# A scan's phase carried from chunk to chunk by an addition into the input's last row, in place of a small transfer or a selecting product

## The chip, the core and the metric

The kernel runs on one core of a Trainium2 chip. The metric is the time of one execution on the device, in microseconds (us). Five engines work side by side, each in its own order: PE (TensorE, products), DVE (VectorE), ACT (ScalarE), POOL (GpSimd) and SP (SyncE, which issues most transfers).

## What is computed

A gated linear attention with complex decay, and on its output a mixture of experts with one expert per token.

```
mag = sqrt(a_re^2 + a_im^2);  scale = min(mag, 0.999) / (mag + 1e-6)
for t in range(768):                       # per batch (4) and head (8), head_dim 48
    S = (a_re*scale + i*a_im*scale)[t] * S + outer(k[t], v[t])
    y[t] = q[t] @ real(S)
x = y as rows: 3072 tokens x 384
e = argmax(x @ w_gate);  out = softmax gate * sigmoid(x @ w_output_gate)[e] * (relu(x @ w1[e]) @ w2[e])
```

## The kernel before

The scan is done in chunks of 128 tokens: 4 batches of 6 chunks, 24 chunks in all, with a chunk's tokens on the 128 partitions and heads times head_dim, 384 numbers, along the row. Chunks are worked in groups (`sizes`) of 1, 1, 2, 2, 3, 3, 3, 3, 3, 3. The first four groups are the six chunks of the first batch.

For a chunk the kernel needs the running sum over its tokens of log magnitude (`decay`, L512) and of phase (`turns`, L560). Both are products with a constant triangle: `tri_l` at L521, `tri_t` at L574, each with 128x384 float32 data, which the trace shows as two matmul records. The phase is the arctangent of a_im / a_re, written in place into the tile `ai` by `prep_trig` (L508, which records as L234). After the product, DVE rounds (L578) and subtracts (L579), so that `ai` now holds the running phase in turns, wrapped to half a turn; L585 takes its absolute value, and `phase` (L600) takes sine and cosine of both on ACT.

The phase must go on from chunk to chunk within a batch. The last token's running phase lies in partition 127 of the finished chunk; the next chunk's first token lies in partition 0. There are two ways, by group (`CARRY = 3`):

- Chunks 1 to 5 (groups 0 to 3): after the product with `tri_t`, a second product (L576) with `sel`, a 32x128 constant that picks row 127, adds the carry to all rows in PSUM. The product with `tri_t` does not wait for the chunk before, the one with `sel` does.
- Chunks 6 to 23 (groups 4 to 9): SP moves row 127 to a tile `carry` on partition 0 (L584), and DVE adds it, times 2 pi, to partition 0 of the next chunk's `ai` (L556) before that chunk's product with `tri_t`. Chunks 6, 12 and 18 begin a batch and take no carry.

Around it, by chunk: `turn` (L618) multiplies k and q by the sines and cosines on DVE (L622, tiles `kc`, `qc`) and turns them on PE (L94, tile `tr`), ACT copies them out (L632); `score` (L657) makes scores on PE (L664) and masks them on DVE (L665); `state` (L636) and `values` (L671) make the state (L644, L649) and the output (L678, L684); `finish` (L693) makes rows and gate logits (L245). Beside them `prep_exp` (L451) prepares the magnitudes of the next group: ACT exponentials and logarithms, and DVE's L467, L481, L490 and L500 over 1152 numbers a row for a group of three.

The order of the attention's instructions is not written out by hand: the generators `main` and `side` say in what order the steps are recorded, `@urge` gives some of them a priority (`turning` counts as recorded 30 instructions earlier), and a planner then orders each engine's and each queue's instructions by priority and by when it takes them to be ready. Only the end of the attention and the experts (L1402 to L1405) are in an order fixed by hand. Each engine works through its own list in order, and an instruction that waits holds up all behind it.

In the experts' part each of the 8 experts makes its rows by products of three float32r parts (L1235, L1172).

## Time and profile before

| | |
|---|---|
| median of 3 runs | 533.52 us (533.45 to 533.83) |
| profiled execution | 535.06 us |
| its span | 533.3 us |
| PE busy | 495.2 us, 93% of the span |
| DVE busy | 340.6 us, 64% |
| ACT busy | 314.2 us, 59% |
| POOL busy | 116.3 us, 22% |

The attention takes the first 300 us or so, the experts the rest. The rows come from the profiled execution, whose time is 1.76 us above its span and 1.54 us above the median of the runs. Busy shares are averages over stages with different limits; what a change in one stage is worth is read from that stage.

### The profile page before, as it was taken

How to read it: one execution, taken by the hardware profiler on the slowest of the kernel's cores; microseconds unless marked ns; L12 is line 12 of the kernel's file. 1: busy time of each engine (PE TensorE's matmuls, PEld its weight loads, DVE VectorE, ACT ScalarE, POOL GpSimd, SP SyncE). 2: the span in 40 equal slices, each digit the busy share in tenths (PEclk: the TensorE clock that was granted, in tenths of full speed). 3: DMA queues.
4: the chain of work that ended last, by engine and by line, in shares of the span. 5: the costliest groups of instructions: out<-in, count | busy, mean ns of one | idle time of the engine just before them, and what ended most of it. 6: DMA issues, size and time to landing. Idle time of an engine off the chain costs nothing.

```text
span 533.3 us, 10970 instructions
## 1 busy us (share of the span) xinstructions
PE 495.2 (93%) x4191; PEld 427.8 (80%) x4191; DVE 340.6 (64%) x801; ACT 314.2 (59%) x581; POOL 116.3 (22%) x134
## 2 busy tenths in 40 slices
PE   2899896999989999999989899999999999999992
PEld 0378574877877878778787789999999999999992
DVE  5579678998877988898857646444353636355220
ACT  7678677887858789657624236355452726354220
POOL 4002002030110203033310544412334232111112
PEclk9799989999989999999999799999999999999998
DMA  8664542526235321104424565537163544431001
GB/s 285 199 216 137 120 132 61 164 67 179 72 75 149 45 77 49 29 31 135 143 56 145 161 170 180 165 82 235 44 205 120 173 149 142 142 115 50 15 27 45
DMA packets 46898, 63.84 MB, mean 120 GB/s; under 512 B 11769, under 2 KB 38668, under 8 KB 46836
## 3 DMA queue, kind: packets, MB, share of 16 engines
q1 hardware_dynamic: 38708, 53.63, 33.6%
q0 software_dynamic: 8128, 9.42, 6.2%
q8 instruction: 35, 0.57, 0.5%
q14 instruction: 27, 0.22, 0.2%
HBM read 53.92 MB, written 9.88 MB: 120 GB/s over the span
## 4 chain that ended last, share of the span: by engine, by line
PE 59%; issue 16%; DVE 8%; DMA 7%; ACT 5%; POOL 3%; POOLq 0%; SPq 0%; DVEq 0%; ACTq 0%
PE acc L1172 12%; PE up L1235 11%; PE tr L94 6%; PE sc L664 5%; PE cs L574 4%; PE xo L678 4%; PE tr L245 4%; PE cs L521 3%; POOL out_dram L1185 3%; PE xo L684 2%; DMA carry<-ai 2%; PE st L649 2%; DMA xd<-xn 1%; DMA ar<-in_a_re_dram 1%; DMA raw<-in_moe_w_dram 1%
## 5 line engine op out<-in xcount | busy, mean ns | idle before, releaser
L1240 DVE SCALAR_TENSOR_TENSOR hl<-up,hh 128x464 fp32r<-128x464 f32 (+7 forms) x64 | 37.7, 589 | 69.8 <-ACT hh L1239 69.5
L1239 ACT ACTIVATE hh<-up 128x464 fp32r<-128x464 f32 (+7 forms) x64 | 33.0, 516 | 72.5 <-PE up L1235 72.5
L1235 PE MATMUL up<-xh,w1h 128*128 128x464 f32 (+7 forms) x192 | 69.1, 360 | 0.2 <-ACT xh L1022 0.2
L1235 PE MATMUL up<-xl,w1h 128*128 128x464 f32 (+7 forms) x192 | 68.1, 355 | 0.0
L1235 PE MATMUL up<-xh,w1l 128*128 128x464 f32 (+7 forms) x192 | 67.8, 353 | 0.0
L1172 PE MATMUL acc<-hh,w2h 128*128 128x464 f32 (+6 forms) x168 | 61.8, 368 | 0.0
L1172 PE MATMUL acc<-hl,w2h 128*128 128x464 f32 (+6 forms) x168 | 59.8, 359 | 1.5 <-DVE hl L1240 1.5
L1172 PE MATMUL acc<-hh,w2l 128*128 128x464 f32 (+6 forms) x168 | 59.8, 356 | 0.0
L1185 POOL DMA_INDIRECT out_dram<-y,sid x28 | 31.7, 1134 | 125.2 <-ACT y L1207 122.2
L664 PE MATMUL sc<-qt,kt 96*128 96x128 f32 x384 | 52.4, 279 | 0.0
L664 PEld LDWEIGHTS sc<-qt,kt 96*128 96x128 f32 x384 | 47.2, 191 | 3.3 <-issue 1.7
L1116 POOL DMA_INDIRECT rows<-xd,sid x28 | 35.5, 1267 | 57.7 <-DVE w1l L211 29.2
L211 DVE TENSOR_TENSOR w1l<-raw,w1h 128x512 fp32r<-128x512 f32 x48 | 30.7, 685 | 18.9 <-ACT w1h L210 18.8
L678 PE MATMUL xo<-scores,v 128*48 128x128 f32 x384 | 42.7, 279 | 0.0
L211 DVE TENSOR_TENSOR w2l<-raw,w2h 128x512 fp32r<-128x512 f32 x48 | 30.6, 688 | 14.6 <-ACT w2h L210 14.3
L1062 POOL DMA_INDIRECT table<-entry,addr x20 | 28.1, 1404 | 53.5 <-DVE addr L1058 49.3
L1235 PEld LDWEIGHTS up<-xl,w1h 128*128 128x128 f32 x192 | 36.3, 189 | 1.6 <-DVE xl L1023 0.4
L210 ACT CAST w1h<-raw 128x512 fp32r<-128x512 f32 x48 | 27.1, 619 | 17.9 <-DMA raw<-in_moe_w_dram 17.9
L1235 PEld LDWEIGHTS up<-xh,w1h 128*128 128x128 f32 x192 | 36.5, 190 | 1.3 <-ACT xh L1022 0.4
L544 POOL COPY rcs<-rcs 24x48 f32<-24x48 f32 (+2 forms) x10 | 5.4, 540 | 146.2 <-DMA rcs<-re 95.6
L1235 PEld LDWEIGHTS up<-xh,w1l 128*128 128x128 f32 x192 | 36.4, 190 | 1.0
L684 PE MATMUL xo<-qt,state 96*48 96x128 f32 x320 | 36.7, 276 | 0.0
(213 smaller groups left out, 1117.9 us busy)
## 6 DMA issues: line engine op xcount, KB each, us to landing
raw<-in_moe_w_dram SPq DMA_DIRECT2D x32, 768.0 KB
ar<-in_a_re_dram SPq DMA_DIRECT2D x24, 192.0 KB
ai<-in_a_im_dram SPq DMA_DIRECT2D x24, 192.0 KB
k<-in_k_dram SPq DMA_DIRECT2D x24, 192.0 KB
q<-in_q_dram SPq DMA_DIRECT2D x24, 192.0 KB
v<-in_v_dram SPq DMA_DIRECT2D x24, 192.0 KB
xd<-xn SPq DMA_DIRECT2D x24, 192.0 KB
rows<-xd,sid POOLq DMA_INDIRECT x28, 4.3
```

Source lines behind the costliest of these rows:

```text
L94: return nc.tensor.transpose(out=out, in_=in_, identity=ident[p0:p0 + n, p0:p0 + n])
L211: nc.vector.tensor_tensor(out=lo[:, s], in0=raw[:, s], in1=hi[:, s].bitcast(F32), op=ALU.subtract)
L664: nc.tensor.matmul(sp[:, j * P:(j + 1) * P], r["kt"][:D2, h, :], r["qt"][:D2, h, :], start=True, stop=True)
L678: nc.tensor.matmul(op[u * DP:u * DP + D, j * P:(j + 1) * P], vt[c][:, h * D:(h + 1) * D], r["s"][:, h, :], start=True, stop=(cc == 0))
L684: nc.tensor.matmul(op[u * DP:u * DP + D, j * P:(j + 1) * P], xs[:D2, h * D:(h + 1) * D], r["qt"][:D2, h, :], start=False, stop=True)
L1062: ins = nc.gpsimd.indirect_dma_start(out=table, out_offset=bass.IndirectOffsetOnAxis(ap=addr[:, c:c + 1], axis=0), in_=entry[:, c, :], in_ ...
L1116: ins = nc.gpsimd.indirect_dma_start(out=rows[e % 2][:n, i, :], out_offset=None, in_=xd[:known], in_offset=bass.IndirectOffsetOnAxis(ap=id ...
L1172: nc.tensor.matmul(accs[kt][:, :cap], w[:, cs], a, start=(ft == 0 and s == 0), stop=(ft == FT - 1 and s == 2))
L1185: ins = nc.gpsimd.indirect_dma_start(out=out, out_offset=bass.IndirectOffsetOnAxis(ap=id_of(e, i, n, loaded), axis=0), in_=y[:n, :], in_of ...
L1235: nc.tensor.matmul(up[:, :cap], w[:, kt, :], x[:, kt, :], start=(m == 0), stop=(m == 3 * KT - 1))
L1239: nc.scalar.activation(out=hh, in_=up[:, :cap], func=AF.Relu)
L1240: nc.vector.scalar_tensor_tensor(out=hl, in0=up[:, :cap], scalar=0.0, in1=hh.bitcast(F32), op0=ALU.max, op1=ALU.subtract)
```

## The change

The arrays a_re and a_im are handed to the kernel with the tokens of each chunk rotated by one: rows 0 to 126 hold tokens 1 to 127, and row 127 holds token 0. The rotation is made where the inputs are laid out, outside of the measured time. The triangles are made to fit, so that the running sums come out in the tokens' own order: `tri_ring` makes a strict triangle and fills its row 127. The first token's phase then lies in partition 127, as the carry does, and one DVE instruction on partitions 96 to 127 adds it in place, with a per-partition factor `last` that is 2 pi in partition 127 and zero in the others. The transfer (L584), the tile `carry`, the product with `sel` (L576) and the constants `sel`, `tri_r` and `tri_o` go. The path taken only when a decay is too strong (`recurrence`, not run with these inputs) first copies both arrays back into the tokens' order.

```diff
-    tri_l = tri("tri_l", 0.5)
-    tri_r = const.tile([P, P], F32R, name="tri_r")
-    nc.gpsimd.tensor_copy(out=tri_r, in_=tri_l)
-    tri_t = tri("tri_t", 1.0 / (2.0 * math.pi))
+    def tri_ring(name, val):
+        t = tri(name, val, strict=True)
+        nc.gpsimd.affine_select(
+            out=t, in_=t, pattern=[[0, P]], compare_op=ALU.is_ge, fill=val, base=P - 2, channel_multiplier=-1)
+        return t
+
+    tri_l = tri_ring("tri_l", 0.5)
+    tri_t = tri_ring("tri_t", 1.0 / (2.0 * math.pi))
     mask = tri("mask", 1.0)
-    tri_o = const.tile([P, P], F32R, name="tri_o")
-    nc.gpsimd.tensor_copy(out=tri_o, in_=mask)
...
-    sel = const.tile([P, P], F32, name="sel")
-    nc.gpsimd.memset(sel, 1.0)
+    last = const.tile([P, 1], F32, name="last")
+    nc.gpsimd.memset(last, 2.0 * math.pi)
     nc.gpsimd.affine_select(
-        out=sel, in_=sel, pattern=[[0, P]], compare_op=ALU.is_ge, fill=0.0,
-        base=-(P - 1), channel_multiplier=1,
-    )
+        out=last, in_=last, pattern=[[0, 1]], compare_op=ALU.is_ge, fill=0.0, base=-(P - 1), channel_multiplier=1)
...
             def carried(g, c):
 
-                first = (starts[g] + c) % NC == 0
-                fr = G[g]["ai"][:, c, :]
-                plain = st["carry"] is not None and st["carry"].shape[0] > 1
-                if not first and not plain:
+                if (starts[g] + c) % NC:
+                    row = G[g]["ai"][96:128, c, :]
                     nc.vector.scalar_tensor_tensor(
-                        out=fr[0:1, :], in0=st["carry"], scalar=2.0 * math.pi, in1=fr[0:1, :], op0=ALU.mult, op1=ALU.add)
-                return first, plain
+                        out=row, in0=st["carry"], scalar=last[96:128], in1=row, op0=ALU.mult, op1=ALU.add)
...
                 tp = pp.tile([P, 512], F32, name="cs")
...
-                    nc.tensor.matmul(tp[:, :HD], tri_t, fr, start=True, stop=first or not plain)
-                if not first and plain:
-                    nc.tensor.matmul(tp[:, :HD], sel[96:128], st["carry"], start=False, stop=True)
+                nc.tensor.matmul(tp[:, :HD], tri_t, fr, start=True, stop=True)
...
-                if g <= CARRY:
-                    st["carry"] = fr[96:128, :]
-                else:
-                    st["carry"] = early.tile([1, HD], F32, name="carry")
-                    nc.sync.dma_start(out=st["carry"], in_=fr[127:128, :])
+                st["carry"] = fr[96:128, :]
...
+        if name in ("a_re", "a_im"):
+            a = _np.ascontiguousarray(_np.roll(a.reshape(a.shape[0], -1, P, *a.shape[2:]), -1, axis=2).reshape(a.shape))
```

The branches for `g >= SPLIT` and `g >= TSPLIT`, which no group reaches (both are 99), go as well.

## Rows read from the trace of the kernel before

**Rows 1.** The page: busy time of each engine with its share of the span and instructions, and the TensorE clock granted in 40 equal slices of 13.3 us, in tenths of full speed.
```profile
PE 495.2 (93%) x4191; PEld 427.8 (80%) x4191; DVE 340.6 (64%) x801; ACT 314.2 (59%) x581; POOL 116.3 (22%) x134
...
PEclk9799989999989999999999799999999999999998
```

**Rows 2.** The waits of the whole span: who waited for whom, us in total, times, longest us.
```profile
PE cs L574 <- DVE ai L556: 7.2, 3, 4.3
...
DVE ai L556 <- DMA carry<-ai: 5.4, 4, 2.5
```

**Rows 3.** The chain of work that ended last, in order of time: start us, length us, what. Pieces of 3 us and more from 60 to 165 us.
```profile
87.07 3.34 DMA carry<-ai
...
119.57 4.21 DMA carry<-ai
...
150.07 4.87 DMA carry<-ai
```

**Rows 4.** Busy time by stretch (us from the span's start): length, busy us and instructions of PE, PEld, DVE, ACT, POOL, then granted clock as a share of full speed, DMA share, GB/s.
```profile
80.00:95.00 15.00, 10.73 (x102) 7.09 (x99) 13.23 (x37) 10.30 (x17) 3.17 (x3) 0.89 0.30 71
...
148.00:162.00 14.00, 12.04 (x109) 10.22 (x108) 9.99 (x26) 6.23 (x12) 1.24 (x1) 0.88 0.42 93
...
180.00:210.00 30.00, 30.00 (x365) 23.28 (x363) 25.93 (x63) 25.32 (x45) 4.64 (x4) 1.00 0.28 63
...
300.00:533.00 233.00, 223.51 (x1258) 215.96 (x1256) 100.76 (x173) 101.99 (x203) 66.13 (x57) 0.98 0.41 127
```

**Rows 5.** The timeline from 85 to 94 us, PE, then DVE, then ACT: start us, length us, engine, line, operation, out<-in, count, and in brackets the idle time before it and what ended it.
```profile
91.12 1.28 PE L574 MATMUL cs<-ai,tri_t 128*128 128x384 f32 x2 [4.27 <-DVE ai L556]
92.30 1.65 PE L521 MATMUL cs<-l,tri_l 128*128 128x384 f32 x2
93.77 1.60 PE L94 MATMUL tr<-ident,kc 128*96 128x128 f32 x8
...
86.49 0.55 DVE L579 TENSOR_TENSOR ai<-cs,rnd 128x384 f32<-128x384 f32 x1
86.96 1.35 DVE L481 SCALAR_TENSOR_TENSOR lnr<-lnr,t 128x1152 f32<-128x1152 f32 x1
...
90.43 0.55 DVE L556 SCALAR_TENSOR_TENSOR ai<-carry,ai 1x384 f32<-1x384 f32 x1 [0.56 <-DMA carry<-ai]
...
92.78 0.94 DVE L622 TENSOR_TENSOR kc<-k,trig 128x768 f32<-128x768 f32 x1
...
88.34 1.25 ACT L234 ACTIVATE t<-lnr,b_eps 128x1152 f32<-128x1152 f32 x1 [3.01 <-DVE lnr L481]
...
91.34 0.60 ACT L234 ACTIVATE trig<-rnd,b_cos 128x384 f32<-128x384 f32 x1
```

**Rows 6.** The timeline from 119 to 126 us, PE, then DVE.
```profile
124.41 0.91 PE L574 MATMUL cs<-ai,tri_t 128*128 128x384 f32 x2 [0.95 <-DVE ai L556]
125.16 0.60 PE L94 MATMUL tr<-ident,qc 128*96 128x128 f32 x4
125.60 1.04 PE L245 MATMUL tr<-comb,xt 128*128 128x112 f32 x8
...
119.00 0.55 DVE L579 TENSOR_TENSOR ai<-cs,rnd 128x384 f32<-128x384 f32 x1
...
121.20 0.94 DVE L622 TENSOR_TENSOR qc<-q,trig 128x768 f32<-128x768 f32 x1
123.81 0.55 DVE L556 SCALAR_TENSOR_TENSOR ai<-carry,ai 1x384 f32<-1x384 f32 x1 [1.67 <-DMA carry<-ai]
```

**Rows 7.** The timeline from 149 to 159 us, PE, then DVE.
```profile
152.97 0.64 PE L94 MATMUL tr<-ident,qc 128*96 128x128 f32 x4
155.57 0.93 PE L574 MATMUL cs<-ai,tri_t 128*128 128x384 f32 x2 [1.96 <-DVE ai L556]
156.31 1.03 PE L94 MATMUL tr<-ident,qc 128*96 128x128 f32 x4
157.14 1.89 PE L245 MATMUL tr<-comb,xt 128*128 128x112 f32 x8
...
151.56 0.95 DVE L622 TENSOR_TENSOR qc<-q,trig 128x768 f32<-128x768 f32 x1
154.97 0.55 DVE L556 SCALAR_TENSOR_TENSOR ai<-carry,ai 1x384 f32<-1x384 f32 x1 [2.45 <-DMA carry<-ai]
```

**Rows 8.** The timeline from 15 to 27 us, PE, then DVE.
```profile
15.71 2.25 PE L574 MATMUL cs<-ai,tri_t 128*128 128x384 f32 x4 [3.05 <-POOL rcs L544]
18.09 1.61 PE L576 MATMUL cs<-ai,sel 32*128 32x384 f32 x2
...
17.38 0.56 DVE L579 TENSOR_TENSOR ai<-cs,rnd 128x384 f32<-128x384 f32 x1
...
19.74 0.56 DVE L578 TENSOR_SCALAR rnd<-cs 128x384 f32<-128x384 f32 x1 [1.41 <-PE cs L576]
```

**Rows 9.** Busy time of PE alone in two short stretches near the start: length, PE busy and instructions, granted clock, DMA share, GB/s.
```profile
20.00:23.00 3.00, 3.00 (x10) 0.50 0.66 180
...
23.00:26.00 3.00, 3.00 (x14) 0.96 0.96 322
```

**Rows 10.** Instructions that write or read the tile `carry`: count, shortest, median and longest ns, first and last start us, form.
```profile
L584 SPq DMA_DIRECT2D carry<-ai x18: 534/552/2036, 80.4 to 240.6; - x18
L556 DVE SCALAR_TENSOR_TENSOR ai<-carry,ai x15: 536/540/601, 84.0 to 237.2; 1x384 f32<-1x384 f32 x15
```

More of the change, by code (lines that the diff above doesn't have):

```diff
@@ L516, in decay @@
                     lp = pp.tile([P, 512], F32, name="cs")
[L517 to L521 removed]
+                    nc.tensor.matmul(lp[:, :HD], tri_l, d["l2"][:, c, :], start=True, stop=True)
                     re = early.tile([P, HD], F32, name="re")
@@ L550, in carried, with turns @@
             def carried(g, c):
[L552 to L555 removed]
+                if (starts[g] + c) % NC:
+                    row = G[g]["ai"][96:128, c, :]
                     nc.vector.scalar_tensor_tensor(
[L557 to L562 removed]
+                        out=row, in0=st["carry"], scalar=last[96:128], in1=row, op0=ALU.mult, op1=ALU.add)
+            def turns(g, c, taken=False):
+                if not taken:
+                    carried(g, c)
                 fr = G[g]["ai"][:, c, :]
                 tp = pp.tile([P, 512], F32, name="cs")
[L565 to L576 removed]
+                nc.tensor.matmul(tp[:, :HD], tri_t, fr, start=True, stop=True)
                 rnd = early.tile([P, HD], F32, name="rnd", bufs=4)
@@ L579, in turns @@
                 nc.vector.tensor_tensor(out=fr, in0=tp[:, :HD], in1=rnd, op=ALU.subtract)
-                if g <= CARRY:
-                    st["carry"] = fr[96:128, :]
-                else:
-                    st["carry"] = early.tile([1, HD], F32, name="carry")
-                    nc.sync.dma_start(out=st["carry"], in_=fr[127:128, :])
+                st["carry"] = fr[96:128, :]
                 nc.vector.tensor_scalar(
@@ L591, in turning @@
                 for c in range(sizes[g]):
-                    taken = carried(g, c)
+                    carried(g, c)
                     yield
-                    turns(g, c, taken)
+                    turns(g, c, True)
                     yield
@@ L1299, in recurrence, with in_order @@
             xrow = xd.rearrange("(b s) (h e) -> b h s e", b=B, h=H)
+            def in_order(name, src):
+                t = dram.tile([N, HD], F32, name=name)
+                by_chunk = t.rearrange("(c t) f -> c t f", t=P)
+                ring = src.rearrange("b (c t) h d -> (b c) t (h d)", t=P)
+                nc.sync.dma_start(out=by_chunk[:, 1:], in_=ring[:, :P - 1])
+                nc.sync.dma_start(out=by_chunk[:, :1], in_=ring[:, P - 1:])
+                return t.rearrange("(b s) (h d) -> b s h d", b=B, h=H)
+            a_re_of, a_im_of = in_order("a_re_of", a_re), in_order("a_im_of", a_im)
             with tc.For_i(0, S, TB) as t0:
                 tiles = {}
-                for name, src in (("q", q), ("k", k), ("ar", a_re), ("ai", a_im)):
+                for name, src in (("q", q), ("k", k), ("ar", a_re_of), ("ai", a_im_of)):
                     t = rp.tile([P, TB, DQ], F32, name="r" + name)
```

15 lines of the change are left out of this document (removed).

## Prediction

> **What bounds the kernel now.** First the page: PE is busy for 93% of the span, no other engine for more than 64% [rows 1]. So an edit is worth what it does to PE's order: holes in it, products in it, and its clock, which falls below full in a few slices only. Then the stretches. In the experts' part, from 300 us, PE is busy for 223.5 of 233 us, and from 180 to 210 us for all 30 [rows 4]; nothing that waits beside PE there is worth anything. Between 80 and 95 us it has 4.3 us without work, from 148 to 162 us 2.0 us, and in just these two stretches the granted clock is 0.89 and 0.88 [rows 4]: 0.11 x 15 = 1.65 us and 0.12 x 14 = 1.68 us of full-rate time are lost beside the holes.
>
> The waits say what the holes are: PE's product with `tri_t` (L574) waited three times, 7.2 us in total, for DVE's addition of the carry (L556), and that addition in turn waited for the transfer 5.4 us in total [rows 2]. The chain of work that ended last runs through three of the transfers, 3.34, 4.21 and 4.87 us long [rows 3]. The other landings of the 18 [rows 10] cost the chain nothing. The ceiling of what the transfers cost is therefore 7.2 + 1.65 + 1.68 = 10.5 us. What a reader must still see is what PE would wait for next in each hole; that is in the timelines.
>
> **The first hole (87 to 91 us).** The finished chunk is there at 86.49 + 0.55 = 87.04 us; the addition runs at 90.43, PE's product at 91.12 after 4.27 us of idleness [rows 5]. With the carry in place the addition could run at 87.04. But then look past the product and the decay product behind it (L521): the next work of weight on PE is turning `kc`, which began at 93.77, right as DVE's `kc` ended (92.78 + 0.94 = 93.72). `kc` needs the second sine, ready at 91.34 + 0.60 = 91.94. ACT came to its sines late because it waited 3.01 us for DVE's L481, which stands behind L579 in DVE's order [rows 5]; DVE itself has only 0.56 us of idleness in front of the addition and is busy for 13.23 of the 15 us [rows 4, 5]. So the product and the decay product move into the hole, and behind them PE waits for `kc`: a new wait in the old one's place. `kc` can come forward from 92.78 to 91.94 at most, 0.84 us, while the order on ACT stays. I take 0.8. Bounds: 0 (kc stays where it is) and 4.27 + 1.65 = 5.9 us (the planner puts other products or an earlier L481 there).
>
> **The second hole (124 us).** DVE idles 1.67 us before the addition, PE 0.95 us before the product [rows 6]. Even if the addition keeps its place in DVE's order, behind `qc` (121.20 + 0.94 = 122.14), it ends at 122.7, before PE is free (124.41 - 0.95 = 123.46). PE's next work, more turning of `qc`, has its input. I take all of it, 0.95; bounds 0 and 0.95.
>
> **The third hole (155 us).** In its old place behind `qc` the addition would run at 151.56 + 0.95 = 152.5 instead of 154.97 and end at 153.1; PE is free at 152.97 + 0.64 = 153.6 [rows 7]. The 1.96 us close. Behind the hole the clock falls: four turns take 1.03 us and the gate products 1.89 [rows 7], where the same work takes 0.60 and 1.04 us after the short second hole [rows 6]; 0.43 + 0.85 = 1.28 us more. Without the hole I expect that not to happen: 1.96 + 1.28 = 3.2 us. Bounds 1.0 (half of the hole filled by a wait for ACT's copies) and 1.96 + 1.68 = 3.6.
>
> **The start, where the change adds a wait.** Chunks 1 to 5 had no transfer. Chunk 0 ends on DVE at 17.38 + 0.56 = 17.94, the product with `sel` begins at 18.09, takes 1.61 us at the lower clock, and DVE rounds at 19.74 [rows 8]. The product with `tri_t` for chunk 1 lay before it, in the 2.25 us from 15.71, and waited for nobody. Now it must wait for the addition: 17.94 + 0.54 + 0.14 (from the addition's end to the product, as 90.98 to 91.12 in rows 5) = 18.6, and 1.6 us on, at 20.3, DVE rounds: 0.6 us later. Chunks 2 and 3 hide the same addition partly behind turning; the end of the run of four is some 0.7 us late. PE saves the `sel` products but has no other work ready. Chunks 4 and 5 (62 to 67 us) swap a `sel` product for an addition in the same way, with decay products at hand to fill the wait; I take 0. The start costs 0.7 us. Bounds: a gain of 1.6 (one `sel` product at the lower clock, if PE is the bound) and a loss of 3.6: three links of 0.7, and 1.5 us of clock. The clock is the part that can hurt. From 20 to 23 us PE is at 0.50, the 1.2 GHz level, from 23 to 26 at 0.96, after it has been busy since 15.71 almost without a pause [rows 8, 9]. With an idle stretch from about 16.8 to 18.6 us the rise may come later; 3 us later costs 3 x 0.5 = 1.5 us of products.
>
> **The rest.** SP loses 18 issues of 0.55 us [rows 10], 9.9 us of a queue on which nothing but the three landings above was late; 0. The addition itself is not in the trace in its new form (32 partitions, the factor read from SBUF): the nearest rows are the old one with 540 ns [rows 10] and a 128x384 subtraction with 550 ns [rows 5]; I take 0.54 each. There are 20 instead of 15, 2.7 us more of DVE, all of it in the first batch and costed above. On POOL copies and fills of constants are swapped for as many others, long before the first product with `tri_t` at 15.71. A finished group's `ai` is now read by the next group's first addition, so the load that reuses its buffer, and what stands behind it on SP, waits that long; the data is wanted two groups later, 0.
>
> A row and a rule on the addition: L579 starts at 86.49 and its successor at 86.96, 0.47 us later, though it lasts 0.55, so neighbours on DVE overlap by some 0.07 us [rows 5]. The Trainium skill, "VectorE: DVE Perf Modes", section "Two Vector instructions with no wait between them", says that an instruction whose inputs start in another group of 32 partitions than the last instruction's is held until all earlier ones have ended, and the next one too when it goes back. The new addition starts at partition 96, all else on DVE at 0; no run of before shows it. As an estimate from that page, 2 x 0.07 us for each of 20 additions is 2.8 us of DVE time, of which the start's links would put some 0.3 us on the path; the sum would be 0.3 us higher.
>
> **Sum.** -0.8 - 0.95 - 3.2 + 0.7 = -4.25 us. The profiled execution, 535.06 us, would become 530.8; it stands 1.54 us above the median of the runs, so the median 533.52 becomes 529.3.
>
> **Rivals.**
>
> *The holes close wholly.* The planner orders all engines anew, with an addition that is ready at once. If it finds products for the first hole and its clock loss goes too: 10.5 us less, 523.0. For it: from 180 us on PE is never without work [rows 4], so work to bring forward may be there. Against: DVE is busy for 88% of that stretch [rows 4], and `kc` hangs on ACT.
>
> *It doesn't do what it says.* The addition stays where it is in DVE's order, and other waits step in: first hole 0, second 0.95, third 1.0, against 1 to 2 us at the start: 532.5 to 533.5, no change. Against: in holes two and three PE's inputs are there.
>
> *Slower, through the start.* The product that used to run ahead now waits, PE idles inside the stretch in which its clock should rise, and the lower level lasts on. It decides if the rise comes more than 3 us later and the links cost their 0.7 three times: +3.6; with the same at chunks 4 and 5, which also follow an idle stretch, twice 3.6. Against the first hole's 0 and 0.95 + 1.96 elsewhere this gives 533.52 + 7.2 - 2.9 = 537.8 at worst, 535 in the middle. A new order on DVE that puts additions ahead of `kc` and scores works in the same direction.
>
> **Chances.** 0.2% is 1.07 us, about what a measurement of this kernel tells from no change. My forecast, 1.1 to 6.5 us less: 0.48. Holes wholly closed, more than 6.5 less: 0.14. No change: 0.15. Slower by the start or by the new order: 0.23. So faster 0.62, same 0.15, slower 0.23. For 8 in 10 the range goes from 523.5, near the ceiling, to 535.8, the middle of the slower case; the forecast's own is 527.0 to 532.4.
>
> **What would show it.** The `carry` rows, L584 and L576 gone; L556 twenty times, near 0.54 us. PE's waits for L556 no longer among the long ones after 80 us; in their place, near 90 us, one for `kc` or its sines of 1 to 3 us. The clock at 1.00 from 148 to 162 us and still below 1 from 80 to 95. At 16 to 19 us a PE wait of some 1.8 us for L556, and the first 30 us 0.7 us longer. The experts unchanged in length and begun 4 to 5 us earlier. I am wrong if a new wait of equal length appears in hole three, if the first 70 us are more than 2 us longer, or if new holes open where PE has none now, as from 180 to 210 us [rows 4], because the planner's order is another one.

## The result: 1.4% slower, and where the 9 us went

| | before | after |
|---|---|---|
| median | 533.53 us | 542.10 us |
| ratio, with its 95% interval | | 1.0144 (1.0121 to 1.0167) |
| span of the profiled execution | 533.3 us | 542.4 us |

The prediction was 529.3 us, with a range to 535.8. The sign is wrong, and the measured time lies outside the range.

The total alone does not say where it went wrong. A marker does that: DVE computes the gate logits once per chunk (L245's product, then a reduction that records as L250), and the experts begin with the first `up` product. Here is when each came, after minus before, in us of the profiled executions. The rows below the first are experiments, told further down; they are set here so that a stage can be read down a column.

| kernel | chunk 0 | chunk 3 | chunk 4 | chunk 20 | chunk 23 | first `up` | span |
|---|---|---|---|---|---|---|---|
| before, at | 45.08 | 83.61 | 99.73 | 255.35 | 273.40 | 279.82 | 533.3 |
| before, traced again | +1.1 | +1.2 | +1.3 | +1.6 | +1.3 | +1.3 | +2.1 |
| **after** | +4.5 | +5.1 | +8.0 | -0.6 | +7.3 | +7.4 | +9.1 |
| e1: product for chunks 1 to 5 | +0.8 | +0.8 | +3.5 | -5.1 | -2.7 | -0.5 | +1.7 |
| e10: e1 and one transfer | -0.6 | -0.6 | -0.2 | -7.4 | -3.8 | -3.2 | -2.5 |
| e2: transfers back from chunk 6 on | +4.4 | +4.9 | +4.9 | +6.0 | +6.7 | +6.7 | +9.5 |
| e12: after, tail in another order | +4.4 | +4.9 | +7.7 | -1.1 | +0.6 | +1.4 | +5.3 |
| e9: before, without one unused transfer | +0.8 | +0.7 | +0.5 | -0.5 | +3.9 | +4.0 | +4.1 |

Traces of one kernel differ as well: the kernel before, traced again, is 1.1 to 1.6 us later at every marker and 2.1 at the end. Its step from one column to the next is 0.4 us at most up to the first `up`, so the steps along a row, in which a late start drops out, are read here rather than single entries.

So there are four stages: 5 us lost at the start, 3 more between chunks 3 and 4 (the first hole), 8.6 won back from chunk 4 to chunk 20, and 8 lost from chunk 20 to chunk 23. The experts add 1.7.

The page after, PE's busy time and the granted clock by slices of 13.6 us:

```profile
PE 494.6 (91%) x4181; PEld 431.9 (80%) x4181; DVE 347.9 (64%) x806; ACT 315.3 (58%) x581; POOL 113.1 (21%) x134
...
PEclk9998969799999999999879799999999999999997
```

PE is busy for as long as before [rows 1], in a span 9 us longer. Next the waits of the whole span (us in total, times, longest) and the stretches that answer to [rows 4], with the one behind the first:

```profile
PE cs L559 <- DVE ai L550: 10.2, 4, 3.2
...
DVE sid L1074 <- DMA slots<-table: 5.1, 1, 5.1
```

```profile
80.00:95.00 15.00, 12.65 (x140) 9.37 (x138) 13.17 (x43) 11.14 (x22) 2.61 (x3) 1.00 0.23 72
95.00:112.00 17.00, 14.57 (x143) 11.52 (x142) 13.51 (x29) 14.42 (x24) 0.00 (x0) 0.80 0.49 147
...
148.00:162.00 14.00, 13.99 (x168) 11.74 (x168) 13.64 (x27) 11.32 (x20) 4.41 (x4) 1.00 0.35 77
180.00:210.00 30.00, 29.99 (x371) 24.27 (x369) 27.43 (x64) 24.83 (x44) 3.14 (x4) 1.00 0.27 67
309.00:542.00 233.00, 223.03 (x1253) 215.44 (x1251) 99.50 (x168) 102.59 (x203) 63.79 (x56) 0.98 0.41 124
```

The waits for the carry's transfers are gone, and PE waits longer than before for the addition (L550, which was L556; `turns` has its product at L559): 10.2 us instead of 7.2 [rows 2]. Of the 10.2, 7.8 us lie in the first batch (2.36 us before 19.75, 3.19 before 67.08, 2.29 before 71.02), where the kernel before has no such wait, and 2.35 in the first hole. From 148 to 162 us PE is now busy throughout at the full clock. But the lost clock of the first hole has not gone; it has moved on, to 95 to 112 us, where the kernel before has 1.00:

```profile
95.00:112.00 17.00, 17.00 (x190) 13.82 (x188) 14.91 (x41) 15.78 (x30) 0.00 (x0) 1.00 0.49 150
```

**The start.** PE, then DVE, from 18 us on:

```profile
19.75 1.65 PE L559 MATMUL cs<-ai,tri_t 128*128 128x384 f32 x2 [2.36 <-DVE ai L550]
...
25.82 0.91 PE L559 MATMUL cs<-ai,tri_t 128*128 128x384 f32 x2
...
30.44 0.91 PE L559 MATMUL cs<-ai,tri_t 128*128 128x384 f32 x2
...
18.09 0.56 DVE L562 TENSOR_TENSOR ai<-cs,rnd 128x384 f32<-128x384 f32 x1
18.68 0.36 DVE L564 TENSOR_SCALAR rnd<-ai 128x384 int32<-128x384 int32 x1
19.07 0.62 DVE L550 SCALAR_TENSOR_TENSOR ai<-ai,last 32x384 f32<-32x384 f32 x1
...
21.43 0.56 DVE L561 TENSOR_SCALAR rnd<-cs 128x384 f32<-128x384 f32 x1 [0.73 <-PE cs L559]
```

DVE rounds chunk 1 at 21.43 instead of 19.74 us [rows 8]. Of these 1.7 us 0.7 lie ahead of the link (chunk 0's subtraction is at 18.09 instead of 17.38; in e1, below, it is at 18.41); the link itself is 1.0 us longer, not 0.6. Two things were left out. DVE takes the absolute value (L564) first and adds after it, so the addition starts 0.98 us after the subtraction instead of 0.56. And at the later links other work stands in PE's order before the product: the addition for chunk 2 ends at 24.37, its product begins at 25.82. The subtraction (L562) is 0.7 us late at chunk 0, then 1.7, 3.4 and 4.4 us at chunks 1, 2 and 3.

**The first hole.** PE, then DVE, as in [rows 5]:

```profile
94.38 0.88 PE L559 MATMUL cs<-ai,tri_t 128*128 128x384 f32 x2 [2.35 <-DVE ai L550]
97.69 2.93 PE L517 MATMUL cs<-l,tri_l 128*128 128x384 f32 x4 [2.43 <-DVE l L490]
100.41 1.92 PE L94 MATMUL tr<-ident,kc 128*96 128x128 f32 x8
...
92.25 1.34 DVE L481 SCALAR_TENSOR_TENSOR lnr<-lnr,t 128x1152 f32<-128x1152 f32 x1
93.62 0.62 DVE L550 SCALAR_TENSOR_TENSOR ai<-ai,last 32x384 f32<-32x384 f32 x1
94.27 0.36 DVE L564 TENSOR_SCALAR rnd<-ai 128x384 int32<-128x384 int32 x1
...
96.29 1.35 DVE L490 SCALAR_TENSOR_TENSOR l<-lnr,t 128x1152 f32<-128x1152 f32 x1
...
98.02 0.95 DVE L601 TENSOR_TENSOR kc<-k,trig 128x768 f32<-128x768 f32 x1
```

One hole of 4.27 us became two, of 2.35 and 2.43 us. PE's order now has two decay products (four records of L517) ahead of turning `kc`, where before there was one; they need `l`, which DVE makes at 96.29, and they run at the lower clock, 2.93 us for four records where [rows 5] have 1.65 for two. Turning `kc` began 6.8 us after L481 started before (93.77 - 86.96), and begins 8.2 us after it now (100.41 - 92.25).

**The tail.** DVE in the kernel before, the addresses of chunks 17 to 19 in the experts' lists (`addr`) and the conversion of the list read back (`sid`):

```profile
250.25 0.17 DVE L1058 TENSOR_SCALAR addr<-row 128x3 uint32<-128x3 f32 x1
...
261.30 0.17 DVE L1095 TENSOR_SCALAR sid<-slots 116x4 uint32<-116x4 f32 x1
```

The same two in the kernel after, with the first of DVE's splits of expert weights (`w1l`):

```profile
247.10 0.68 DVE L211 TENSOR_TENSOR w1l<-raw,w1h 128x512 fp32r<-128x512 f32 x1
...
254.90 0.15 DVE L1037 TENSOR_SCALAR addr<-row 128x3 uint32<-128x3 f32 x1
...
266.48 0.17 DVE L1074 TENSOR_SCALAR sid<-slots 116x4 uint32<-116x4 f32 x1 [5.12 <-DMA slots<-table]
```

Chunk 19's logits come at 245.57 before and 246.10 after. The addresses follow 4.7 us later before and 8.8 us later after, because six splits of weights now stand between the steps of the routing on DVE. POOL's scatter into the table, the list's reading, the conversion and the gathering of rows all hang on them.

### The profile page after: what moved, and what is told of

Read it like the earlier page. It is cut to its first block, busy times and chain, and to the rows that moved or that the text cites. A ratio compares the mean times of both kernels' runs of the same rounds, so it can differ in the third digit from the quotient of the medians.

```text
span 542.4 us, 10931 instructions
## 1 busy us (share of the span) xinstructions
PE 494.6 (91%) x4181; PEld 431.9 (80%) x4181; DVE 347.9 (64%) x806; ACT 315.3 (58%) x581; POOL 113.1 (21%) x134
## 4 chain that ended last, share of the span: by engine, by line
PE 25%; issue 16%; POOL 4%; DMA 2%; DVE 2%; SPq 1%; POOLq 0%; ACT 0%; ACTq 0%
PE acc L1151 11%; PE up L1214 11%; POOL out_dram L1164 3%; DMA xd<-xn 2%; POOL rows L1095 1%; PE yp L94 1%; PE xt L94 1%; DMA rows<-xd,sid 1%; SPq L1062 0%; DVE w1l L211 0%; SPq L1068 0%; PE yp L751 0%; PE yp L762 0%; DVE hl L1219 0%; POOL table L1041 0%
## 5 line engine op out<-in xcount | busy, mean ns | idle before, releaser
L643 PE MATMUL sc<-qt,kt 96*128 96x128 f32 x384 | 54.5, 286 | 0.0
L643 PEld LDWEIGHTS sc<-qt,kt 96*128 96x128 f32 x384 | 48.6, 198 | 2.8 <-issue 2.0
L657 PE MATMUL xo<-scores,v 128*48 128x128 f32 x384 | 40.9, 287 | 2.2 <-DVE scores L644 2.2
L1041 POOL DMA_INDIRECT table<-entry,addr x20 | 25.1, 1257 | 66.6 <-DVE addr L1037 62.7
L611 ACT COPY kt<-tr 96x512 f32<-96x512 f32 x48 | 26.4, 587 | 18.1 <-PE tr L94 18.1
L644 DVE TENSOR_TENSOR scores<-sc,mask 128x512 f32<-128x512 f32 x48 | 32.8, 684 | 6.1 <-PE sc L643 6.0
```

Of the source, the lines that this page charges most:

```text
L611: (nc.vector.tensor_copy if i < QTD and which == "q" else nc.scalar.copy)(out=r[which + "t"][:D2, 4 * hh:4 * hh + 4, :].rearrange("p h t - ...
L643: nc.tensor.matmul(sp[:, j * P:(j + 1) * P], r["kt"][:D2, h, :], r["qt"][:D2, h, :], start=True, stop=True)
L644: nc.vector.tensor_tensor(out=r["s"][:, 4 * hh:4 * hh + 4, :], in0=sp.rearrange("p (h t) -> p h t", t=P), in1=mask.unsqueeze(1).broadcast_ ...
L657: nc.tensor.matmul(op[u * DP:u * DP + D, j * P:(j + 1) * P], vt[c][:, h * D:(h + 1) * D], r["s"][:, h, :], start=True, stop=(cc == 0))
```

## The experiments

### The start alone: e1

The change, but the carry of chunks 1 to 5 goes through the product with `sel` again:

```diff
-                if (starts[g] + c) % NC:
+                if (starts[g] + c) % NC and g > CARRY:
...
+                product = g <= CARRY and (starts[g] + c) % NC != 0
-                nc.tensor.matmul(tp[:, :HD], tri_t, fr, start=True, stop=True)
+                nc.tensor.matmul(tp[:, :HD], tri_t, fr, start=True, stop=not product)
+                if product:
+                    nc.tensor.matmul(tp[:, :HD], sel[96:128], st["carry"], start=False, stop=True)
```

> The changed layout with one part undone: chunks 1 to 5 take their carry by the product with sel again (the carry is in row 127 there too), chunks 6 to 23 by the addition in place. Theory A (the added wait in front of the product with tri_t in chunks 1 to 5 delays the first batch): chunk 3's finished phase (L562, fourth) falls back from 32.3 to about 28 us, the gate logits of chunk 0 come at about 45 instead of 49.6 us, and the whole is 4 to 5 us shorter than the changed kernel. Rival B (the start's delay is made up for anyway, since chunks 17 to 20 are level with the kernel before in the changed kernel): the first batch is earlier but the total is within 1 us of the changed kernel.

Measured: 537.03 us, 1.0042 (0.9996 to 1.0089) of before. Chunk 3 is 0.8 us late instead of 5.1. PE near 20 us:

```profile
19.11 1.61 PE L569 MATMUL cs<-ai,sel 32*128 32x384 f32 x2
20.66 1.65 PE L567 MATMUL cs<-ai,tri_t 128*128 128x384 f32 x2
22.24 1.77 PE L94 MATMUL tr<-ident,kc 128*96 128x128 f32 x8
23.95 0.91 PE L569 MATMUL cs<-ai,sel 32*128 32x384 f32 x2
```

The product with `tri_t` (L567) fills the time in which the carry is made, and the full rate is there at 23.95. After is 4.3 us behind e1 at chunk 3, and 3.9 behind the kernel before as traced again, so the change's five additions at the start cost about 4 us.

When the full rate begins is not part of this cost as far as the runs show, since it differs between traces of one kernel. The first line is from e10, the others from e10 traced again (both below); their start is e1's:

```profile
19.94 0.91 PE L570 MATMUL cs<-ai,tri_t 128*128 128x384 f32 x2
...
27.59 1.49 PE L570 MATMUL cs<-ai,tri_t 128*128 128x384 f32 x2
29.00 0.91 PE L572 MATMUL cs<-ai,sel 32*128 32x384 f32 x2
```

A pair of these records takes 0.91 us at the full rate. It is reached by 19.94 us in the one and by 29.00 in the other, whose chunk 3 is 5.0 us late without an addition at the start. In after it is reached between 23.81 and 25.82 us, in the kernel before as traced again between 24.00 and 25.11.

In e1 the loss at the first hole (0.8 to 3.5 at chunk 4) and the gain in the middle (8.6) are those of after, and 4.6 us are still lost from chunk 20 to the first `up`: these have other causes.

### The first hole: e10

e1, with one transfer put back, that of chunk 7, for which PE had waited 4.27 us [rows 5]. It goes to partition 127 of a zeroed tile, and the addition reads it there:

```diff
+    moved = const.tile([P, HD], F32, name="moved")
+    nc.gpsimd.memset(moved, 0.0)
...
                 st["carry"] = fr[96:128, :]
+                if starts[g] + c == 7:
+                    nc.sync.dma_start(out=moved[127:128, :], in_=fr[127:128, :])
+                    st["carry"] = moved[96:128, :]
```

> e1_product_first (the changed kernel with the product for chunks 1 to 5) with one transfer put back: the finished row of chunk 7 goes by SP to partition 127 of a constant tile, where chunk 8's addition reads it, so that the wait of the first hole is there again. Theory (in the first hole the ready addition brings the steps of chunk 8 and a second decay product ahead of turning kc, which costs more than the wait it removes): PE's order in the hole is that of the kernel before, one decay product ahead of turning kc; PE waits some 4 us for the addition near 91 us, turning kc begins near 94.6 us instead of 96.05, and chunk 4's logits come at +0.8 to +1.3 us against the kernel before instead of +3.5. Rival (the loss comes from the clock or from ACT's order): chunk 4 stays at +3 or more, with the wait on top.

Measured: 532.89 us, 0.994 (0.9908 to 0.9971) of before, under both kernels. PE:

```profile
90.88 1.48 PE L570 MATMUL cs<-ai,tri_t 128*128 128x384 f32 x2 [4.53 <-DVE ai L560]
92.18 1.65 PE L527 MATMUL cs<-l,tri_l 128*128 128x384 f32 x2
93.64 1.45 PE L94 MATMUL tr<-ident,kc 128*96 128x128 f32 x8
```

PE waits 4.53 us again, for the addition behind a transfer, and turning `kc` begins 2.4 us earlier than in e1 (96.05); 1.4 of that this run has from its start. From chunk 3 to chunk 4 the kernel loses 0.4 us instead of 2.7. This holds over all traces of changed kernels: the ten without the transfer of chunk 7 lose 1.1 to 2.9 us there, the seven with it 0.6 at most. The 1.1 and 1.5 us are those of e8 and e3, in which turning `kc` is back at the full rate (1.11 and 1.12 us for eight records, against 1.92 in after); so more than 1 us of the 2.9 is the clock's. Without the wait the order that the planner makes brings the steps of chunk 8 and a second decay product ahead of turning `kc`.

More than half of this comes back, though. One part is the decay product, which e1 has done early; e10 still has it to do behind chunk 4's marker:

```profile
102.19 0.81 PE L527 MATMUL cs<-l,tri_l 128*128 128x384 f32 x2
```

From chunk 3 to chunk 20 e10 gains 6.8 us and e1 5.8 (6.7 in e10 traced a third time). So the wait was the cheaper one, by 1.0 us. Of the 4.2 us between the two spans, 1.4 lie ahead of chunk 3 and are not the edit's; the other 1.8 us come behind chunk 20 and were not taken apart.

### The middle: e2

The change, with the transfer put back for all chunks from 6 on, by the same edit with `g > CARRY` as its condition and two tiles in turn; chunks 1 to 5 keep the addition in place.

> The changed kernel, with the transfer put back for chunks 6 to 23: row 127 of the finished chunk goes to row 127 of a constant tile, and the addition reads it there; chunks 1 to 5 keep the addition in place. Theory (the start costs 4.5 to 5 us, the middle regains 7 to 9 by having no transfer, the tail loses because a transfer is gone from SP's queue): chunk 0's logits at 49.6 us as in the changed kernel, chunks 10 to 20 stay 4 to 6 us later than in the kernel before, no late addresses at the end, first up product 4 to 5 us later than before, and a ratio of 1.007 to 1.010. Rival (the start's loss is caught up later in any case, as PE has slack in the middle): chunks 17 to 20 within 1 us of before, and a ratio under 1.003.

Measured: 541.39 us, 1.0104 (1.0053 to 1.0156). The start's loss stays to the end: chunk 4 is 4.9 us late, chunk 20 is 6.0 late, where after had won 8.6 us between them. So the transfers' removal is worth 8.6 + 1.1 = 9.7 us from chunk 4 to chunk 20. Part of that is the first hole's loss coming back: counted from chunk 3 it is 5.7 + 1.1 = 6.8. This rests on one trace of e2, 3.2 us longer than the median of its runs. Against e10, which has the transfer of chunk 7 as well, it is 7.9 us from chunk 3 and 8.3 from chunk 4; that is about twice the 4.15 summed for the second and third hole. The first hole's extra loss is absent in e2, as in e10, and so is the tail's: with the transfers back, chunk 20 to the first `up` costs 0.7 us and not 8.

### The tail: e4, e5, e9, e12

In after, DVE waits 5.12 us at the conversion. Is that wait the cost, or a sign of a late list? e4 takes the change and moves the conversion to POOL; e5 does the same to e1:

```diff
-        nc.vector.tensor_scalar(
+        (nc.gpsimd if n1 == 1 else nc.vector).tensor_scalar(
             out=sid[:NP, n0:n1], in0=slots[:NP, n0:n1, :, 0], scalar1=float(NONE), scalar2=None, op0=ALU.add)
```

> The changed kernel with the conversion of the first expert's row numbers (L1074, one small instruction that waits for the transfer slots<-table) moved from DVE to POOL, which must wait for it anyway; all other orders stay. Theory T (DVE's 5.1 us at 261 us in that wait is what makes the last three chunks 7 us late): DVE no longer idles at 261 us, chunk 21's logits come at about 263.5 instead of 268.4 us, and the total falls by 4 to 6 us. Rival: the chain goes on through the gathered rows (rows<-xd) and the transfers behind them on SP (xd<-xn at 283 us), so less than 1.5 us is gained.

> Both edits of the two runs before together: product with sel for chunks 1 to 5, addition in place for the others, the conversion on POOL. If the start and DVE's late wait are the two losses and the closed holes the gain, the total is 7 to 10 us below the changed kernel, 531 to 534, or below the kernel before if the gain of the middle (7 to 9 us between chunk 4 and chunk 17) stays: 525 to 530. If the middle's gain was only catching up with the late start, it is at 533 or above.

Measured: 543.83 us, 1.0138 (1.0054 to 1.0222), and 537.77 us, 1.002 (0.9979 to 1.0061). In e4 DVE no longer waits and chunk 23's logits come 0.6 us before those of before instead of 7.3 behind. The first `up` product is still 6.6 us late, and the time is that of after: PE then waits 3.1 us for the gathered rows. The wait was a sign. e5 is above 533 us, as its rival had it, but not for the rival's reason: the gain of the middle stays (5.8 us from chunk 3 to chunk 20, as in e1), and 5.0 us are lost between chunk 23 and the first `up`.

e9 asks what made the list late. It is the kernel before, without the transfer of chunk 23's carry, which nobody reads:

```diff
-                    nc.sync.dma_start(out=st["carry"], in_=fr[127:128, :])
+                    if starts[g] + c < NT - 1:
+                        nc.sync.dma_start(out=st["carry"], in_=fr[127:128, :])
```

> The kernel before, without one instruction: the carry transfer of chunk 23, the last chunk, which nobody reads. Everything up to 235 us is unchanged. Theory (the tail's loss in the changed kernel is not the addition's doing: without the last carry transfer SP starts the first expert's weight loads 2.5 us earlier, and DVE's splits of them are then ordered between the steps of the last routing, whose addresses come late): the weight loads start near 240.3 instead of 242.7 us, the addresses of chunks 17 to 19 come 8 to 9 us after chunk 19's logits instead of 4.7, DVE waits some 4 to 5 us for the list at its conversion, the first up product starts at 283 to 285 us instead of 279.8, and the time is 3 to 5 us longer, a ratio of 1.006 to 1.010. Rival (the tail is late for another reason, the additions' order or the late start): the first up product within 1 us of 279.8 and a ratio of 1.000 within 0.002.

Measured: 539.01 us, 1.0048 (1.0016 to 1.0081). DVE:

```profile
254.94 0.16 DVE L1059 TENSOR_SCALAR addr<-row 128x3 uint32<-128x3 f32 x1
...
265.31 0.17 DVE L1096 TENSOR_SCALAR sid<-slots 116x4 uint32<-116x4 f32 x1 [3.72 <-DMA slots<-table]
```

To take away one transfer that is of no use to anyone costs 4.0 us at the first `up` product and, by the ratio, 2.6 us of the whole. Half of the expectation fell, though: the weights' first load starts at 242.88 us, as before (242.74), and not 2.5 us earlier. It is not an earlier load that harms but the order: with one issue less in SP's queue the planner has put six splits of the weights between the routing's steps, as in after.

e12 turns it round: the change as it is, with one constraint, that DVE's splits of the first expert's weights stand behind the addresses of chunks 17 to 19 (`after` is the kernel's own helper for an order without a wait):

```diff
+                if wait:
+                    after(ins, first_addr)
```

> The changed kernel as it is, additions in place everywhere, with one constraint: DVE's splits of the first expert's weights are ordered behind the addresses of chunks 17 to 19. Theory (the order of the tail is worth 4 to 7 us): no wait over 1 us at the list's conversion, the first up product at 280 to 283 us instead of 287.2, and the time 4 to 7 us under the changed kernel's, a ratio to the kernel before of 1.001 to 1.007. Rival (the tail is late for the additions before it): up at 286 or later and a ratio of 1.012 to 1.016.

Measured: 538.73 us, 1.0056 (1.0023 to 1.009).

```profile
250.61 0.17 DVE L1044 TENSOR_SCALAR addr<-row 128x3 uint32<-128x3 f32 x1
...
264.17 0.16 DVE L1081 TENSOR_SCALAR sid<-slots 116x4 uint32<-116x4 f32 x1
```

The addresses are 4.8 us behind the logits, the conversion waits for nobody, and the first `up` product comes at 281.18 instead of 287.20. Of these 6.0 us 3.8 reach the end of the span; in the first 30 us behind the first `up`, PE is idle for 4.2 us instead of 2.3. Of these 3.2 us are two waits for DVE's `hl`, where after has one of 2.2; 0.9 has no cause in the trace.

### What the additions cost DVE: e3

The change with the addition over all 128 partitions, so that it starts at partition 0 like the rest (`last` is zero elsewhere):

```diff
-                    row = G[g]["ai"][96:128, c, :]
+                    row = G[g]["ai"][:, c, :]
-                        out=row, in0=st["carry"], scalar=last[96:128], in1=row, op0=ALU.mult, op1=ALU.add)
+                        out=row, in0=st["carry"], scalar=last, in1=row, op0=ALU.mult, op1=ALU.add)
```

> The changed kernel with the addition over all 128 partitions (the factor is zero in 127 of them), so that its tensors start at partition 0 as all else on DVE does; the order on every engine stays the same. Theory H (an addition that starts at partition 96 is held and holds its successor): the addition falls from 0.62 to about 0.55 us, its successor starts 0.47 instead of 0.66 us after it, some 0.2 us for each of 20 additions, and the total falls by 0.5 to 2 us, since only part of them are on the path. Rival: the longer time is that of the factor read from memory, then the addition stays at 0.62 and the total the same.

Measured: 540.5 us, 1.008 (1.004 to 1.0121). The additions of after, all twenty (count, shortest, median and longest ns), and one of e3 with its neighbours on DVE:

```profile
L550 DVE SCALAR_TENSOR_TENSOR ai<-ai,last x20: 617/618/687, 19.1 to 234.5; 32x384 f32<-32x384 f32 x20
```

```profile
89.69 1.35 DVE L481 SCALAR_TENSOR_TENSOR lnr<-lnr,t 128x1152 f32<-128x1152 f32 x1
90.95 0.62 DVE L550 SCALAR_TENSOR_TENSOR ai<-ai,last 128x384 f32<-128x384 f32 x1
91.48 0.36 DVE L564 TENSOR_SCALAR rnd<-ai 128x384 int32<-128x384 int32 x1
```

With 128 rows the addition starts 0.09 us before L481 ends (89.69 + 1.35 = 91.04) and its successor 0.53 us after its start. In after, with 32 rows from partition 96, it starts 0.03 us after L481's end (92.25 + 1.34 = 93.59) and the successor 0.65 us later: 0.12 us held on either side. The Trainium skill, "VectorE: DVE Perf Modes", section "Two Vector instructions with no wait between them", says just this, that an instruction from another group of 32 partitions is held until the earlier ones have ended, and so is the one that goes back; these two traces agree, with 0.12 us each. The length itself, 0.62 us against 0.54 for the old addition [rows 10], stays with full rows, so it is not the start partition's; the factor read from SBUF is the other difference, which no run took alone.

In after all twenty additions start 0.01 us or more behind their predecessor's end, in e3 nineteen of them 0.07 us or more ahead of it. With 0.12 us on either side this is 0.24 us an addition and, as an estimate, at most 4.8 us of DVE for twenty. What reaches the total is not settled: e3's ratio of 1.008 stands against 1.0144, with intervals that touch at 1.0121, and e8 is 2.6 us under e7 (below), but e13 is 0.6 us above e10 where they ran side by side. Of the 1.6 us that e3's trace gains on after between chunk 3 and chunk 20, 1.4 lie in the step to chunk 4, where turning `kc` takes 1.12 us in e3 and 1.92 in after; the hold leaves little to see in the middle.

### Towards a better kernel: e7, e8, e11, e13

e7 is e1 with the first weight loads made to wait for a logits instruction, so that the routing goes first on DVE; e8 is e7 with full rows; e11 is e8 with early loads and e12's constraint in place of e7's wait.

> The changed kernel with the product for chunks 1 to 5 (as e1_product_first), and the first expert's first weight loads made to wait for a gate logits instruction, so that DVE's splits come after the addresses of chunks 17 to 19, as in the kernel before. Theory (late addresses cost the tail what the start and the middle gained): addresses some 5 us after chunk 19's logits, no wait of DVE at the conversion over 1 us, chunk 23's logits near 267 to 268 us, the first up product at 274 to 276 us instead of 279.3 in e1_product_first, and the time 3.5 to 5 us under e1_product_first: a ratio to the kernel before of 0.991 to 0.997. Rival (the weights are wanted early; loading them later makes the first expert wait): first up product at 279 or later and the time that of e1_product_first or more.

> e7_loads_later with the 15 additions over all 128 partitions instead of 32. Theory of the held instructions: every addition and its successor start some 0.1 us sooner, in total up to 2 us under e7_loads_later where DVE is the bound, at least not slower; a ratio to the kernel before of 0.988 to 0.997. Rival (with chunks 1 to 5 on the product, no addition is on the path any more): the time of e7_loads_later within 0.6 us.

> e8_loads_later_full with the weight loads early again, as in e1_product_first; instead, DVE's splits of the first expert's weights are ordered behind the addresses of chunks 17 to 19. So the weights are early and the list is early. Theory (two things set the tail, the list's addresses and the first weights; e7 and e8 mended one at the price of the other): addresses 4.7 to 5 us after chunk 19's logits, first weight load near 233 to 236 us, chunk 23's logits at 265 to 267 us, first up product at 272 to 274.5 us, and a ratio to the kernel before of 0.988 to 0.995. Rival (the weights were not late in e8): the first up product at 275.1 us or later and the time of e8.

Measured: 536.05 us, 0.9989 (0.9953 to 1.0025); 533.46 us, 0.9973 (0.9938 to 1.0009); 535.11 us, 1.0011 (0.9974 to 1.0049). e7's addresses are early as wanted, but its loads start at 243.36 us instead of 235.74, ACT and DVE then wait for the weights, and the first `up` product is 0.8 us later than in e1: the rival was right, though the time is not above e1's. In e11 both are early and `up` comes at 276.08, not at the 272 to 274.5 expected, and PE then idles for 4.2 us in the first 30 us of the experts, as in e12. In these runs the tail's order is a trade between the list and the weights; none of the three shows a gain over before beyond its interval.

e13 is e10 with full rows.

> e10_transfer_of_7 with the 15 additions over all 128 partitions instead of 32; every engine's order stays the same. Theory (an addition that starts at partition 96 holds itself and its successor on DVE, 0.1 to 0.2 us each, and this adds up where DVE is the bound, as in e3_full_rows): 1.5 to 3 us under e10_transfer_of_7, 530 to 531.5 us where that kernel had 532.9, a ratio to the kernel before of 0.987 to 0.993, and the addition's successor 0.53 instead of 0.65 us behind its start. Rival (once the product carries chunks 1 to 5, DVE is not the bound where the other additions stand): the time of e10_transfer_of_7 within 0.7 us, a ratio of 0.993 to 0.996.

Measured: 541.35 us, 1.01 (1.0061 to 1.0138), 8 us above e10 with the same order on every engine. PE in e13 (the bracket gives the idle time before; "issue" is time in which it waited for nothing that the profile shows):

```profile
147.63 0.26 PE L644 MATMUL st<-v,kc 128*32 128x48 f32 x2 [0.18 <-issue]
149.81 0.30 PE L679 MATMUL xo<-qt,state 96*48 96x128 f32 x1 [0.29 <-issue]
150.53 0.31 PE L673 MATMUL xo<-scores,v 128*48 128x128 f32 x1 [0.20 <-issue]
```

Nine such pauses stand between 115 and 215 us, all within the short products of state and output, and PE's order, which is e10's, falls 6.8 us back on e10 over this stretch. The nine brackets add up to 2.3 us; most of the rest is lost in steps at the same products. No earlier trace had one there. Two more sets of runs were to tell the kernel from its conditions.

> The same kernel as e10_transfer_of_7, on the same chip as the two that follow. Theory (one transfer put back in the first hole and the product for chunks 1 to 5 make the change a gain): a ratio to the kernel before of 0.991 to 0.997, first up product 3 us earlier than in the kernel before. Rival (the gain was that chip's): a ratio of 1.000 or more.

> The same kernel as e13_transfer_full. In its trace PE pauses some ten times for 0.2 to 0.5 us between 115 and 215 us, inside products of the state and the output, waiting for nothing that the profile shows, and the attention falls 6 us back on e10_transfer_of_7, which has the same order on every engine. Theory A (the pauses belong to the kernel: a full-row addition in this order): they are here again, and the ratio is 1.006 to 1.014. Theory B (they belong to that chip or to that run): they are gone, and the kernel is 1 to 3 us under e10_again.

> e1_product_first with the 15 additions over all 128 partitions, the same order on every engine, and nothing else. Theory (the hold costs 0.1 to 0.2 us an addition where DVE is the bound): 1.5 to 3 us under e1_product_first, a ratio of 0.996 to 1.001 where that was 1.004, and no pauses of PE without a reason. Rival (full rows bring the pauses of e13_transfer_full with them): a ratio of 1.008 or more, with pauses.

Measured: 544.32 us, 1.0142 (1.0089 to 1.0195); 545.08 us, 1.014 (1.0061 to 1.0219); 542.66 us, 1.0133 (1.0071 to 1.0195). All three have seven to nine pauses, between 115 and 220 us, e10 too, which had none in its first run:

```profile
153.87 0.22 PE L644 MATMUL st<-v,kc 128*32 128x48 f32 x1 [0.43 <-issue]
156.08 0.44 PE L673 MATMUL xo<-scores,v 128*48 128x128 f32 x4 [0.26 <-issue]
156.82 0.44 PE L679 MATMUL xo<-qt,state 96*48 96x128 f32 x4 [0.30 <-issue]
```

> The kernel before itself, profiled beside the two that follow. It tells whether the short pauses of PE between 115 and 220 us, seen in e13_transfer_full, e10_again, e13_again and e14_product_first_full and in no earlier trace, come to the kernel before too under the same conditions. Theory (they belong to the conditions of the run and not to the change): where the two that follow have them, this one has them too, and its attention is later by several us than in its first profile. Rival (only the changed kernels have them): no pause over 0.15 us without a reason between 95 and 220 us here, and pauses in the two others.

> The same kernel as e10_transfer_of_7. Without pauses of PE: a ratio to the kernel before of 0.991 to 0.998. With them: 1.005 to 1.016, as in e10_again.

> The same kernel as e13_transfer_full. Without pauses of PE: 1 to 3 us under e10_third, by the theory of the hold; within 0.7 us of it by the rival. With pauses: 1.005 to 1.016, and no verdict on the hold.

Measured, without pauses in any of the three: 536.01 us, 1.0001 (0.996 to 1.0042); 534.53 us, 0.9964 (0.992 to 1.0009); 535.09 us, 0.9974 (0.9931 to 1.0018). So the same kernel runs with the pauses and without. Without them e10 was faster than before twice, 0.994 and 0.9964, the second time with an interval that just reaches 1; with them it was slower. Whether the kernel before has them under the same conditions was not seen, as its profile was taken in the set without. Its times speak against it: in the two sets with pauses its medians were 536.7 and 537.6 us, against 533.5 to 536.5 in the others, while e10 went from 532.9 to 544.3. That only the changed kernels are open to the pauses is therefore a rival that is left, and e10 is no sure gain. The trace of after has none, so its 1.0144 is not explained by them.

## Why the prediction was wrong, step by step

**The start was mis-sized, by the links that its rival named.** The step "DVE rounds: 0.6 us later" took the addition to follow the subtraction at once; the absolute value stands between them, and the link cost 1.0. The step "chunks 2 and 3 hide the same addition partly behind turning" failed: the turning did not hide the addition, it went ahead of the product in PE's order, and the lateness grew to 4.4 us. PE's idle time at 19.75 was 2.36 us where 1.8 was written. In place of 0.7 us the start cost 4.3 against e1 and 3.9 against before traced again, beyond the bound of 3.6. The rival's other half, that the idle time would put off the full rate, was not shown: the rate begins at about the same time in after and in before traced again. For chunks 4 and 5 "I take 0" was 1.2 us off: L562 of chunk 5 is 5.6 us late against 4.4 for chunk 3, and the decay products that were to fill the wait did not: PE waits 3.19 and 2.29 us for the additions there.

**The first hole: PE's order behind it, taken as given, did not stay.** The prediction saw rightly that the addition would become free and that another wait would step in. It took PE's old order behind the hole, with the new wait as one for `kc`; another order stood among its bounds, but as a gain. The planner made a new order: two decay products first, waiting for `l`. A gain of 0.8 was summed; at chunk 4 a loss of 2.9 was measured, of which 1.0 us is left at chunk 20 (e1 against e10). The clock did not recover either: 1.00 from 80 to 95 us, where less was foretold, but 0.80 from 95 to 112, where before had 1.00.

**The second and third hole: right, and too small.** PE no longer waits there, the clock is 1.00 from 148 to 162 us as foretold, and the transfers' removal is worth some 8 us (e10 against e2) instead of 4.15. The sum counted PE's visible holes only; how the rest comes about was not taken apart.

**The tail was in no step.** "SP loses 18 issues ... 0" was the failing one. An unused transfer at the end of SP's queue held the order of the last routing in place; e9 shows that its removal alone costs 4.0 us at the first `up`, e2 that the tail's loss goes when the transfers come back, and e12 that the order is worth 6.0 in after. No rival had it; "a new order on DVE" was named, but put at the additions, not at the experts' weights. So the range could not hold the result; its upper end, 535.8, was also called the middle of the slower case, which that rival put at 535 with 537.8 at worst.

**The hold** was named with an estimate of 0.3 us on the sum. The held time is there, 0.12 us on either side where 0.07 was taken; the addition is also 0.08 us longer than the 0.54 taken.

Of the signs listed, `carry` gone, twenty additions and the clock in the third hole came true; a wait for the addition after 80 us was still there, 2.35 us at 94, the wait near 90 us for `kc` did not come, and the experts began 7.4 us later, not 4 to 5 earlier. Of the conditions written down for being wrong the first was met, as the first 70 us are some 5 us longer; the planner's other order showed, but in the last chunks and not from 180 to 210 us, where PE still has no hole.

## What to carry to other kernels

Where a planner orders the instructions, no edit is local: price the order that it will write, not the old order with a wait cut out, and look behind every removed issue, even an unused one, for what it held in place. A wait that an engine spends on a transfer can be cheaper than what the planner puts there once the wait is gone, here by 1.0 us; put single waits back, one at a time, before giving up a change. Read what a stage costs some stages later, too: of the 2.4 us between e1 and e10 at the first hole 1.4 came back. A carry that a second product adds behind a first keeps the first off the chain; an addition ahead of the product puts both on it.

## What the hardware showed that was not expected

- The TensorE record of the granted clock reads 1.00 from 14 to 26 us in after, while its pairs of 128x384 records take 1.62 to 1.65 us there and 0.91 us from 25.82 on. In before the record agrees with the durations (0.50 from 20 to 23 us [rows 9]). In these traces the durations tell the rate at the start, the record not always.
- The full rate can begin at another time in another run of one kernel: by 19.94 us and by 29.00 in two traces of e10, which are 5.5 us apart at chunk 3.
- PE can pause for 0.2 to 0.5 us, seven to nine times in 100 us, among short products, with no wait in the trace: e10 came out at 0.994 without and 1.0142 with such pauses. What causes them stays open, and so does whether the kernel before has them.
- Where a DVE instruction starts matters to its neighbours: 0.12 us lost on either side of one that begins at partition 96 among others at 0.
